# Where an attention's loads stand in its slots, and when the first expert's weights are fetched

## The chip, the cores and the metric

The kernel runs on one core of one Trainium2 chip. The metric is the time of one execution on the device in microseconds (us). TensorE multiplies matrices, VectorE, ScalarE and GpSimd do the rest of the arithmetic, and SyncE issues most of the transfers between DRAM and the on-chip memory, one after the other in the order in which they were written. In the profile they are PE (with PEld for weight loads), DVE, ACT, POOL and SP.

## The reference

Attention over 8 batches, 8 heads, 576 positions and 64 features a head, whose scores have a causal mask and a bias from cumulative sums; then a mixture of 8 experts, where a token takes its own best expert or keeps that of the token before it.

```python
scores = scale * np.matmul(q, k.transpose(0, 1, 3, 2))
bias = -(cum[:, :, :, None] - cum[:, :, None, :])          # cum: running sum of max(s, 0)
scores = np.where(causal, -1000000000.0, scores + np.minimum(bias, 0.0))
attn = np.exp(scores - np.max(scores, axis=-1, keepdims=True))
attn = attn / (np.sum(attn, axis=-1, keepdims=True) + 1e-09)
x = np.matmul(attn, v)                                      # heads side by side: (B, S, 512)
...
e = fresh_e if s == 0 or local_gate[b, s] < 0.5 else prev_e # fresh_e: argmax of x @ w_gate
out[b, s] = p[e] * (np.maximum(x[b, s] @ w1[e], 0.0) @ w2[e])   # 512 -> 1024 -> 512
```

## The kernel before, in words

The order of work is written out by hand: the program's engines run their instructions in the order of the code. The attention takes two heads as one pair (32 pairs in all), and two pairs as one slot, `m` = 0 to 15. A slot does this on TensorE:

- the scores of its two pairs, in three units each (`scores`, line 1128, tile `ps`), each unit followed by an exponential on ScalarE (line 1129, tile `e`);
- half-block products (`values_halves`, line 1197) and the half-block scores of the next slot's two pairs (`scores_halves`, line 1146, tile `ph`), which read q and k of the next slot;
- the products with the values of the first pair (`values`, line 1185, into `po`) and of the second (into `pb`), in two parts each; after each part VectorE takes the reciprocals of the sums (`evacuate`, line 1207, tile `recs`) and scales.

After every fourth slot the finished batches' tokens get their router logits, and in the slots that follow their expert is worked out and GpSimd scatters their rows to a table in DRAM (line 364, `table`). From slot 14 on the experts' first two units of tokens are fetched back from that table (`experts.fetch`, line 583, tile `xq`), and after slot 15 the experts run: layer 1 of unit 0 first (line 782, tile `hp`).

The inputs of a slot are loaded two slots ahead. Slot `m` loads q and k (288 KB each) and v (320 KB each) of the pairs 2m + 4 and 2m + 5: `load_v` (line 1027, tile `va`) and `qk_part` (line 1274, tiles `kb`, `qb`). q and k have four buffers each, v has six. The function `transfers` gives a slot's loads, each under the name of a place. `let_go` issues the load that waits under a place, and holds it until the instruction that ended there is through (`held` adds that as a dependency):

- `e{u}{n}`: the exponential of unit `u` of the slot's first (n = 0) or second (n = 1) pair; `e21` is the last of the slot;
- `h`: after the half-block products, with the slot's last exponential as the instruction that is waited for;
- `x0`, `x1`: the reciprocals of the first pair's two parts; `y0`, `y1`: those of the second pair's.

All of them are issued by SyncE, so one that waits holds up those behind it. Also on SyncE are, in slot 2, a small array `ends` written to DRAM and read back twice into `wend` (lines 1093 and 1095, placed between `x1` and `y0`), four stores of padding rows (line 203), and in slot 14 the fetches of units 0 and 1 (placed after the first pair's scores).

The first expert's first-layer weights are one tile `w1b` of 2 MB, loaded in four quarters of 512 KB (`experts.load(0, 0, i, behind)`, line 573). Quarter `i` is the `i`-th quarter of the contraction of 512, so the first output block of layer 1 needs all four.

Of the kernel before, what the change touches and what calls it, by code (L numbers as in the profile page):

```python
# [23 lines left out]
NPAIR = B * HP  # L24
# [963 lines left out]
def attention(ctx, tc, q, k, v, s, wx, ident, recs, wend, router, experts):  # L988
# [32 lines left out]
    def load_v(n, behind=None):  # L1021

        if n >= NPAIR:
            return
        b, hp = divmod(n, HP)
        va = vs[n] = p_v.tile([P, NB, 2, DH], F32, name="va")
        held(tc, nc.sync.dma_start(va.rearrange("p c h d -> p (c h d)"), v[b, hp].rearrange("p c h d -> p (c h d)")), behind)
# [207 lines left out]
    for g in range(NG - 1):  # L1235
        m = HP * GB // 2 * (g + 1)
# [9 lines left out]
        for c in range(NC):  # L1246
# [3 lines left out]
            i, p = places[c]  # L1250
# [3 lines left out]
    m = NPAIR // 2  # L1254
# [14 lines left out]
    def qk_part(n, what):  # L1269
        def load(behind):  # L1270
            b, hp = divmod(n, HP)
            to = p_in.tile([P, S], F32, name=what + "b")
            ins.setdefault(n, [None, None])["qk".index(what)] = to
            held(tc, nc.sync.dma_start(to, (q, k)["qk".index(what)][b][:, hp]), behind)
        return load

    def v_part(n):
        return lambda behind: load_v(n, behind)

    def transfers(m):  # L1280

        n = 2 * m + NV
        k0, q0, k1, q1 = (qk_part(n + i, x) for i in range(2) for x in "kq")
        if m == 0:
            return {"e11": v_part(4), "h": k0, "x0": q0, "x1": k1, "y0": q1}
        if m == 1:
            return {"e00": v_part(5), "e10": v_part(6), "e20": k0, "e11": q0, "h": k1, "x0": q1, "x1": v_part(7)}
        of = {"e00": v_part(n), "e20": v_part(n + 1), "e11": k0, "h": q0, "x0": k1, "x1": q1} if n < NPAIR else {}
        i = m - NPAIR // 2 + 5
        if 0 <= i < 4:  # L1290
            of["y1"] = lambda behind: experts.load(0, 0, i, behind)
        return of

    waiting = {}

# [4 lines left out]
    for m in range(NPAIR // 2):  # L1300
        pair = 2 * m, 2 * m + 1
        waiting = transfers(m)
        for n in pair:
            for u in range(len(UNITS)):
# [623 lines left out]
```

## Time and profile before

| | |
|---|---|
| median of 3 runs | 692.24 us (689.48 to 693.06) |
| the profiled execution | 693.14 us |
| its span, first to last instruction | 691.2 us |
| granted TensorE clock | 0.998 |
| TensorE busy | 672.4 us (97%) |
| DMA queues: loads (q1), scatters and stores (q0), instructions (q8, q14) | 58.4%, 7.6%, 0.7% of 16 DMA engines' span |

A row of the engine timeline gives the start and the length in us, the engine, the line, the operation, the tiles written and read, the shape, the count, and in brackets how long the engine had been idle and what released it; "issue" there is a wait that no other engine's or transfer's signal ended. A row of the chain (the work that ended last, traced back from the end) gives start, length and what ran. A row of the table by stretches gives the stretch, its length, each engine's busy time and number of instructions in it (in the order PE, PEld, DVE, ACT, POOL), the granted clock, the mean busy share of the 16 DMA engines, and GB/s.

### The profile page before, as it was taken

What the parts mean: (1) busy time and instruction counts of PE and PEld (TensorE: products, weight loads), DVE (VectorE), ACT (ScalarE), POOL (GpSimd) and SP (SyncE); (2) the same over time, 40 slices, a digit from 0 to 9 for tenths busy, and PEclk for the clock granted to TensorE, in tenths of its full rate; (3) what the DMA queues carried; (4) which work ended last, traced back from release to release, by engine and by line L of the source; (5) the groups of instructions that cost most, each with busy time, mean ns of one, the idle gap of its engine ahead of it and who ended that gap; (6) DMA issues with size and microseconds to landing.
All of it is one profiled execution on the core that took longest, in us unless ns stands there. A gap on an engine that the chain in (4) does not pass through costs nothing.

```text
span 691.2 us, 19171 instructions
## 1 busy us (share of the span) xinstructions
PE 672.4 (97%) x7837; PEld 582.7 (84%) x7837; DVE 523.1 (76%) x979; ACT 198.1 (29%) x368; POOL 385.6 (56%) x547
## 2 busy tenths in 40 slices
PE   8999999999999999999999999999999999999995
PEld 7887888878888899999998999999697897779984
DVE  4664867876875797989989997786587786679762
ACT  4554636355332121121211212212121122212121
POOL 3552367777685858647455465645444373525642
PEclk9999999999999999999999999999999999999999
DMA  7664566777668978499848546464987979856001
GB/s 258 194 209 150 165 199 181 228 215 222 178 213 347 328 260 288 131 362 364 285 155 288 193 154 264 129 265 123 362 289 303 409 261 325 267 249 257 31 13 39
DMA packets 54968, 158.18 MB, mean 229 GB/s; under 512 B 11156, under 2 KB 31636, under 8 KB 49111
## 3 DMA queue, kind: packets, MB, share of 16 engines
q1 hardware_dynamic: 47751, 136.52, 58.4%
q0 software_dynamic: 6880, 20.10, 7.6%
q8 instruction: 64, 1.05, 0.6%
q14 instruction: 33, 0.27, 0.1%
q10 hardware_dynamic: 240, 0.25, 0.1%
HBM read 136.21 MB, written 20.85 MB: 227 GB/s over the span
## 4 chain that ended last, share of the span: by engine, by line
PE 90%; DVE 4%; issue 2%; DMA 1%; POOL 1%; ACT 1%; POOLq 0%; DVEq 0%
PE p L692 28%; PE p L688 27%; PE ps L1128 11%; PE po L1185 6%; PE pb L1185 6%; PE hp L782 4%; PE yp L805 2%; PE hp L773 2%; PE lp L231 1%; PE ph L1146 1%; DVE wt L618 1%; PE po L1197 1%; DMA qb<-in_q_dram 1%; PE pb L1197 1%; POOL out_dram L757 1%
## 5 line engine op out<-in xcount | busy, mean ns | idle before, releaser
L692 PE MATMUL p<-w2b,hT 128*128 128x256 f32 (+1 forms) x720 | 165.0, 380 | 3.2 <-DVE w2b L618 2.4
L692 PEld LDWEIGHTS p<-w2b,hT 128*128 128x128 f32 (+1 forms) x720 | 132.8, 187 | 26.1 <-issue 5.2
L688 PE MATMUL p<-xT,w1b 128*128 128x128 f32 (+1 forms) x1280 | 151.1, 275 | 0.9 <-DVE w1b L618 0.9
L688 PEld LDWEIGHTS p<-xT,w1b 128*128 128x128 f32 x1280 | 147.9, 192 | 3.5 <-issue 1.6
L1129 ACT ACTIVATE e<-ps 128x768 f32<-128x768 f32 (+1 forms) x96 | 76.3, 885 | 60.4 <-PE ps L1128 60.4
L757 POOL DMA_INDIRECT out_dram<-y,gi x38 | 45.3, 1191 | 81.7 <-ACT y L716 72.8
L717 ACT ACTIVATE hT<-hT 128x512 f32<-128x512 f32 (+1 forms) x64 | 39.0, 615 | 154.8 <-DVE hT L712 154.8
L716 ACT ACTIVATE y<-y,gi 128x256 f32<-128x256 f32 (+1 forms) x72 | 35.5, 506 | 166.1 <-DVE y L712 154.0
L1128 PE MATMUL ps<-qb,kb 64*128 64x384 f32 (+4 forms) x516 | 76.9, 444 | 0.2 <-ACT e L1129 0.2
L669 POOL TENSOR_TENSOR hT<-hT,hS 128x512 f32<-128x512 f32 (+1 forms) x18 | 26.4, 1467 | 87.4 <-PE p L692 87.3
L1128 PEld LDWEIGHTS ps<-qb,kb 64*128 64x128 f32 x516 | 47.6, 188 | 27.1 <-ACT e L1129 10.4
L692 PE MATMUL p<-wt,hS 128*128 128x256 f32 (+1 forms) x288 | 68.1, 379 | 0.2 <-DVE wt L618 0.2
L364 POOL DMA_INDIRECT table<-xb,idx x54 | 55.7, 1032 | 15.6 <-issue 13.5
L1112 POOL TENSOR_SCALAR_AFFINE_SELECT e<-e 128x128 f32<-128x128 f32 (+1 forms) x96 | 38.8, 417 | 44.2 <-ACT e L1129 43.5
L688 PE MATMUL p<-xS,wt 128*128 128x128 f32 (+1 forms) x512 | 62.4, 275 | 0.0
L692 PEld LDWEIGHTS p<-wt,hS 128*128 128x128 f32 (+1 forms) x288 | 53.7, 187 | 8.9 <-PE p L692 0.6
L688 PEld LDWEIGHTS p<-xS,wt 128*128 128x128 f32 x512 | 59.7, 192 | 0.0
L1185 PE MATMUL pb<-vg,e 128*64 128x66 f32 x1280 | 42.0, 223 | 3.7 <-issue 3.7
L1185 PEld LDWEIGHTS pb<-vg,e 128*64 128x64 f32 x1280 | 39.7, 138 | 4.8 <-issue 4.7
L1185 PE MATMUL po<-vg,e 128*64 128x66 f32 x1280 | 41.4, 223 | 1.1 <-issue 1.1
L1185 PEld LDWEIGHTS po<-vg,e 128*64 128x64 f32 x1280 | 38.9, 138 | 2.5 <-issue 1.3
L1105 DVE TENSOR_TENSOR vg<-va,wk 128x256 f32<-128x256 f32 x64 | 37.7, 652 | 0.0
(290 smaller groups left out, 984.7 us busy)
## 6 DMA issues: line engine op xcount, KB each, us to landing
w2b<-in_w_dram SPq DMA_DIRECT2D x23, 2048.0 KB, 12.2
w1b<-in_w_dram SPq DMA_DIRECT2D x22, 2048.0 KB, 14.0
va<-in_v_dram SPq DMA_DIRECT2D x32, 320.0 KB, 3.5
kb<-in_k_dram SPq DMA_DIRECT2D x31, 288.0 KB, 3.0
qb<-in_q_dram SPq DMA_DIRECT2D x31, 288.0 KB, 4.9
xq<-table SPq DMA_DIRECT2D x60, 130.0 KB, 3.1
w1b<-in_w_dram SPq DMA_DIRECT2D x4, 512.0 KB, 4.7
xq<-table SPq DMA_DIRECT2D x12, 113.8 KB, 12.8
```

The lines of the kernel that those rows point to most:

```text
L364: put = self.nc.gpsimd.indirect_dma_start(out=self.halves, in_=src, element_offset=0, in_offset=None, out_offset=bass.IndirectOffsetOnAxis ...
L688: mm(ps[:, m * h : m * h + h], lhsT=b[:, k, m * P : m * P + P], rhs=a[:, k, :], start=m == 0 and k == 0, stop=m == FK // 2 - 1 and k == n - 1)
L692: mm(ps[:h, : D // 2], lhsT=a[:, k, :], rhs=b[:, k, :], start=k == 0, stop=k == n - 1)
L716: return nc.scalar.mul(to, to, gi[:h, r, 1:2]).ins
L717: return nc.scalar.activation(to, to, Act.Relu).ins
L757: put = nc.gpsimd.indirect_dma_start(out=self.out[:, :], out_offset=bass.IndirectOffsetOnAxis(ap=gi.bitcast(I32)[:m, n, 0:1], axis=0), in_ ...
L782: mm(ps, lhsT=self.ws[ls[0]][0][:, k, c * P : c * P + P], rhs=xT[:, k, :w], start=(k == 0), stop=(k == DK - 1))
L1105: nc.vector.tensor_tensor(vg[:, to].rearrange("p c h e -> p (c h) e")[:, :, :DH], va[:, :c].rearrange("p c h e -> p (c h) e"), wk[:, n, to ...
L1112: nc.gpsimd.affine_select(out=ap, in_=ap, compare_op=Alu.is_ge, fill=0.0, base=base, pattern=n, channel_multiplier=-1)
L1128: mm(ps[:, h, at : at + z - a], lhsT=kb[d, key : key + P], rhs=qb[d, a:z], start=True, stop=True)
L1129: exps[n, u] = nc.scalar.activation(e[:, :, : WIDTH[u]], ps, Act.Exp, scale=scale).ins
L1185: of = mm(po[part][d, j - a, :], lhsT=weights_of(n, c, j, h), rhs=vgs[n % NV][:, c if j < 2 * G1 else G1 + c, h, :], start=(first and i == ...
```

## The change

Only the table in `transfers` changes. A slot's loads are given other places, and the four quarters of the first expert's weights, one in each of the slots 11 to 14 at `y1`, are now all in slot 14, which has no loads of q, k and v.

```diff
         n = 2 * m + NV
         k0, q0, k1, q1 = (qk_part(n + i, x) for i in range(2) for x in "kq")
-        if m == 0:
-            return {"e11": v_part(4), "h": k0, "x0": q0, "x1": k1, "y0": q1}
-        if m == 1:
-            return {"e00": v_part(5), "e10": v_part(6), "e20": k0, "e11": q0, "h": k1, "x0": q1, "x1": v_part(7)}
-        of = {"e00": v_part(n), "e20": v_part(n + 1), "e11": k0, "h": q0, "x0": k1, "x1": q1} if n < NPAIR else {}
-        i = m - NPAIR // 2 + 5
-        if 0 <= i < 4:
-            of["y1"] = lambda behind: experts.load(0, 0, i, behind)
-        return of
+        if m < 2:
+            return {"e21": v_part(n), "h": k0, "x0": q0, "x1": k1, "y0": q1, "y1": v_part(n + 1)}
+        if n < NPAIR:
+            return {"e21": v_part(n), "h": v_part(n + 1), "x0": k0, "x1": q0, "y0": k1, "y1": q1}
+        parts = ("h", "x0", "x1", "y0") if n == NPAIR else ()
+        return {x: lambda behind, i=i: experts.load(0, 0, i, behind) for i, x in enumerate(parts)}
```

On TensorE, VectorE, ScalarE and GpSimd every instruction stands where it stood; only SyncE's queue differs. In an ordinary slot even its order is the same, and what differs is the engine that each load waits for. These are SyncE's rows of slot 4 before (in brackets the semaphores, DMAHW of an earlier transfer, and the engine whose instruction lets the load go: Activation is ScalarE's exponential, DVE VectorE's reciprocal):

```order
L1027 DMA va<-in_v_dram 128x640 [waits DMAHW1_49,Activation_49]
L1027 DMA va<-in_v_dram 128x640 [waits DMAHW2_49,Activation_49]
L1274 DMA kb<-in_k_dram 128x576 [waits DMAHW3_49,Activation_49]
L1274 DMA qb<-in_q_dram 128x576 [waits DMAHW4_49,Activation_49]
L1274 DMA kb<-in_k_dram 128x576 [waits DMAHW5_49,DVE_49]
L1274 DMA qb<-in_q_dram 128x576 [waits DMAHW6_49,DVE_49]
```

And the same six now:

```order
L1027 DMA va<-in_v_dram 128x640 [waits DMAHW1_49,Activation_49]
L1027 DMA va<-in_v_dram 128x640 [waits DMAHW2_49]
L1274 DMA kb<-in_k_dram 128x576 [waits DMAHW3_49,DVE_49]
L1274 DMA qb<-in_q_dram 128x576 [waits DMAHW4_49,DVE_49]
L1274 DMA kb<-in_k_dram 128x576 [waits DMAHW5_49,DVE_49]
L1274 DMA qb<-in_q_dram 128x576 [waits DMAHW6_49,DVE_49]
```

Both v now wait for the slot's one last exponential, and all of q and k for the reciprocals.

In slot 2, where SyncE also has the transfers of `ends`, `wend` and the padding (`table<-pad`), its rows before were these, from the slot's second k on:

```order
L1274 DMA kb<-in_k_dram 128x576 [waits DMAHW2_49,DVE_49]
L1274 DMA qb<-in_q_dram 128x576 [waits DMAHW3_49,DVE_49]
L1093 DMA ends<-ends 64x9 [waits DMAHW4_49,Pool_49]
L1095 DMA wend<-ends 64x288 [waits DMAHW5_49,DMAHW4_49]
L1095 DMA wend<-ends 64x288 [waits DMAHW6_49]
L203 DMA table<-pad 128x260 [waits DMAHW7_49,Pool_49]
```

And now, from the first q on:

```order
L1274 DMA qb<-in_q_dram 128x576 [waits DMAHW1_49,DVE_49]
L1093 DMA ends<-ends 64x9 [waits DMAHW2_49,Pool_49]
L1095 DMA wend<-ends 64x288 [waits DMAHW3_49,DMAHW2_49]
L1095 DMA wend<-ends 64x288 [waits DMAHW4_49]
L1274 DMA kb<-in_k_dram 128x576 [waits DMAHW5_49,DVE_49]
L1274 DMA qb<-in_q_dram 128x576 [waits DMAHW6_49,DVE_49]
L203 DMA table<-pad 128x260 [waits DMAHW7_49,Pool_49]
```

The second k and q moved behind `ends` and the two reads of `wend`, the first of which waits for the transfer of `ends`.

In slot 14, after the fetch of unit 1, SyncE had one quarter left before (the loads of 128x4096 are those of the expert stage):

```order
L583 DMA gi<-table 128x2x2
L573 ISA
L573 DMA w1b<-in_w_dram 128x1024
L556 TENSOR_LOAD a0of
L573 ISA
L573 DMA w1b<-in_w_dram 128x4096
```

Now it has the read of the expert's number (`a0of`) and all four:

```order
L583 DMA gi<-table 128x2x2
L556 TENSOR_LOAD a0of
L573 ISA
L573 DMA w1b<-in_w_dram 128x1024
L573 ISA
L573 DMA w1b<-in_w_dram 128x1024
L573 ISA
L573 DMA w1b<-in_w_dram 128x1024
L573 ISA
L573 DMA w1b<-in_w_dram 128x1024
L556 TENSOR_LOAD a0of
```

The three quarters that stood behind the loads of the slots 11, 12 and 13 have left those places.

## Prediction

> **What bounds the kernel now.** I read the page first, then the engine waits of TensorE, then its timeline at the waits, then counts of its instructions up to them.
>
> ```profile
> PE 672.4 (97%) x7837; PEld 582.7 (84%) x7837; DVE 523.1 (76%) x979; ACT 198.1 (29%) x368; POOL 385.6 (56%) x547
> q8 instruction: 64, 1.05, 0.6%
> PE 90%; DVE 4%; issue 2%; DMA 1%; POOL 1%; ACT 1%; POOLq 0%; DVEq 0%
> ```
>
> TensorE is busy for 672.4 of 691.2 us and holds 90% of the chain that ended last, so the change can win only what makes TensorE wait in the attention (the first 201 us; the experts keep their order). Its waits there are nearly all of one kind:
>
> ```profile
> PE pb L1185 <- issue: 3.7, 6, 1.3
> PE po L1185 <- issue: 1.1, 2, 0.7
> ```
>
> These are eight stalls, 4.8 us in all, inside the products of the values, where no data released the engine ("issue"). Three of them in its timeline (start, us, what, idle before):
>
> ```profile
> 52.98 1.51 PE L1185 MATMUL pb<-vg,e 128*64 128x66 f32 x45 [1.17 <-issue]
> 148.78 1.44 PE L1185 MATMUL pb<-vg,e 128*64 128x66 f32 x42 [1.28 <-issue]
> 197.54 0.86 PE L1185 MATMUL po<-vg,e 128*64 128x66 f32 x22 [0.33 <-issue]
> ```
>
> What they wait for shows in a count. The table by stretches gives TensorE's matmuls and weight loads from the start up to a time (the x after PE and PEld):
>
> ```profile
> 0.00:47.80 47.80, 45.51 (x975) 37.07 (x979) 26.39 (x60) 24.85 (x41) 23.22 (x82) 1.00 0.68 215
> 0.00:51.90 51.90, 49.52 (x1106) 40.88 (x1107) 29.31 (x67) 26.07 (x43) 25.37 (x85) 1.00 0.70 221
> 0.00:60.70 60.70, 57.24 (x1231) 46.72 (x1235) 33.90 (x75) 31.04 (x50) 27.88 (x91) 1.00 0.66 211
> 0.00:143.90 143.90, 139.68 (x3263) 114.57 (x3267) 96.20 (x250) 74.26 (x131) 78.85 (x190) 1.00 0.63 196
> 0.00:147.60 147.60, 143.28 (x3392) 117.96 (x3392) 99.28 (x264) 76.01 (x135) 82.11 (x197) 1.00 0.64 198
> 0.00:197.30 197.30, 190.71 (x4536) 156.76 (x4536) 135.97 (x366) 100.09 (x177) 118.65 (x268) 1.00 0.65 200
> ```
>
> The three stalls come at instructions 2213, 6784 and 9072. The distances, 4571 and 2288, are 18 and 9 times 254. The q8 row has 64 packets in 1.05 MB, 16.4 KB each, for 15,674 matmuls and weight loads: TensorE gets its program in blocks of some 254 of these, each one packet on queue 8, and it stalls at a border whose next block is late. In the DMA view the block's packet starts within 50.6 to 50.7, 146.5 to 146.6 and 195.2 to 195.3 us, and for a block that came in time within 61.2 to 61.3 us:
>
> ```profile
> q8 instruction: 1, 0.02, 58.2%
> q8 instruction: 1, 0.02, 60.5%
> q8 instruction: 1, 0.02, 67.1%
> q8 instruction: 1, 0.02, 63.4%
> ```
>
> TensorE resumed 2.3, 2.2 and 2.3 us after the first three. The block before the stall at 51.8 began at about 47.8 (254 instructions earlier), so its fetch started 2.8 us in: 2.8 + 2.3 is 1.1 us more than the 4.0 us that the block lasted, and 1.17 was measured. From 143.9 it is 2.6 + 2.2 against 3.6: 1.2, measured 1.28. The block that began at 60.7 had its fetch after 0.5 us and no stall. What differs is the traffic of the other queues (last columns: DMA share, GB/s):
>
> ```profile
> 48.10:50.60 2.50, 2.50 (x91) 2.50 (x87) 1.60 (x4) 0.70 (x2) 1.96 (x3) 1.00 0.90 280
> 144.00:146.50 2.50, 2.50 (x110) 2.43 (x101) 2.26 (x11) 1.43 (x4) 2.16 (x6) 1.00 0.87 220
> 61.00:61.20 0.20, 0.20 (x16) 0.19 (x8) 0.00 (x0) 0.00 (x0) 0.00 (x0) 1.00 0.12 46
> ```
>
> The late fetches stood behind 2.5 us of DMA at 90% and 87%; the quick one met 12%. The loads of q, k and v delay TensorE's instructions.
>
> [...] In this trace the borders cost 4.8 us.
>
> **The change, term by term.** Only SyncE's queue has another order; the other engines run the same rows.
>
> *The block fetches of the slots before the last.* The loads stood at the first exponential of a slot, its fourth, fifth and last, and the first two sums. They now start at the last exponential and end with the last sums.
>
> ```profile
> 43.45 4.75 ACT L1129 ACTIVATE e<-ps 128x1024 f32<-128x1024 f32 x6 [0.86 <-PE ps L1128]
> 46.66 0.97 SPq L1027 DMA_DIRECT2D va<-in_v_dram  x2
> 47.72 0.38 SPq L1274 DMA_DIRECT2D kb<-in_k_dram  x1
> 48.23 0.36 SPq L1274 DMA_DIRECT2D qb<-in_q_dram  x1
> ```
>
> In slot 3 the block at 47.8 met four loads issued from 46.66 to 48.23. Now the first v may go at 48.2, where the exponentials end, and moves no byte before the block's fetch is asked for. The backlog falls on the next block, which holds the scores and is long: the one from 51.8 lasts to 60.7, 8.9 us, against 3 + 2.3 that its fetch needs. Seven of the stalls, 4.8 - 0.33 = 4.45 us, lie in these slots. Ends: all 4.45 go, or none. I take it that each leaves 0.2 us, since a block that begins just after the last exponential still meets the two v loads: 7 x 0.2 = 1.4 us. Net -3.05.
>
> *The second k and q of slot 2.* They now stand on SyncE behind the two reads of wend, which wait for a DRAM round trip:
>
> ```profile
> 39.98 0.53 SPq L1093 DMA_DIRECT2D ends<-ends  x1
> 43.31 1.11 SPq L1095 DMA_DIRECT2D wend<-ends  x2
> 44.52 2.04 SPq L203 DMA_DIRECT2D table<-pad  x4
> 47.35 0.58 PE ph L1146 x40
> ```
>
> So k goes at 44.5 (where the first pad went) and q at 45.0; the half blocks' scores of slot 3 (ph) use them from about 47.4, and the stall ahead of them (0.25) that goes makes it 47.1. Landing, by the page's list of issues (KB each, median us):
>
> ```profile
> kb<-in_k_dram SPq DMA_DIRECT2D x31, 288.0 KB, 3.0
> qb<-in_q_dram SPq DMA_DIRECT2D x31, 288.0 KB, 4.9
> w1b<-in_w_dram SPq DMA_DIRECT2D x4, 512.0 KB, 4.7
> ```
>
> By the k row q is there at 48.0, a wait of 0.9 us; by the q row, whose loads stood behind others, at 49.9, 2.8 us. The queue is quiet here, so I take 1.0. The pads move behind them and nobody is near to needing those.
>
> *The second q of the other slots.* It is let go by the last sums (the reciprocal below ends at 115.45) and needed by ph of the next slot:
>
> ```profile
> 115.23 0.22 DVE L1207 RECIPROCAL recs<-pb 128x10 f32<-128x10 f32 x1 [1.13 <-PE pb L1185]
> 120.24 0.58 PE ph L1146 x40
> ```
>
> That is 4.8 us of cover; with 3.0 to land 1.8 us are left. Cost 0.1 us for a slot where the four releases come close together; ends 0 and 5 (a rival below). The v loads, now later by up to 4 us, are used by VectorE at the end of the slot: in slot 3 the values end at 54.5 (52.98 + 1.51), 6.3 us after the last exponential, and a v is to be there in the time of a k (3.0) with another ahead of it (about 1 more): 0.
>
> *The expert's quarters.* Three leave the slots 11 to 13 (that gain is in the first term), and all four go in slot 14:
>
> ```profile
> 183.48 2.54 SPq L583 DMA_DIRECT2D xq<-table  x4
> 187.14 3.06 SPq L583 DMA_DIRECT2D xq<-table  x4
> 191.05 10.44 SPq L573 DMA_DIRECT2D w1b<-in_w_dram  x2
> 201.02 5.38 PE hp L782 x24
> 179.00:180.00 1.00, 1.00 (x10) 0.52 (x8) 1.00 (x3) 1.00 (x3) 0.91 (x1) 1.00 1.00 303
> ```
>
> Their places in slot 14 have passed when SyncE is through with fetching two units' rows at 190.9, so they go together, from 191.3 to about 193. A lone quarter fills the DMA engines at 303 GB/s, so 2.1 MB take 6.9 us from 192.3, to 199.2, and with the scatters that share these engines to about 200.5. The first product of unit 0 (hp, 201.02) needs all four: 0.1 us, ends 0 and 2. The block from 193.7 now meets the burst. Before, with one quarter, its fetch came 1.5 us in and the stall was 0.33. The longest wait for a fetch seen is 2.8 us, which makes a stall of 1.6; at 2.3 it is 1.1. I take 1.1, so +0.8; ends -0.3 and +4 (a rival).
>
> Sum: -3.05 + 1.0 + 0.1 + 0.1 + 0.8 = -1.05 us. The profiled execution took 693.14 us (span 691.2), 0.9 above the median of 692.24; the difference counts from the median: **691.2 us**. The experts are to pass it on, TensorE being the bound there as well.
>
> **Rivals.**
> 1. *All block stalls go and the late loads are in time.* For it: the quick fetch in the quiet stretch. -4.8 + 0.5 = -4.3, or 687.9.
> 2. *The stalls stay and move.* The loads still take the same share of the slot; two v loads stand together where two single ones were, and products of values now meet them. Then only the costs are left: 692.24 + 2.0 = 694.2. [...] Against it: the 12% row.
> 3. *The burst holds the instructions.* If the block from 193.7 stands behind all four quarters, it is fetched at 199.2 and there at 201.5, against 197.2 needed: 4.3 us instead of 1.1, 694.4. [...] No row here has such a burst beside a fetch.
> 4. *Slower: the second q is late in every slot.* If it takes over 4.8 us to land, ph waits in the nine slots where no router product lies before it. At 5.4 us: 9 x 0.6 = 5.4, or 696.6. For it the 4.9 of the q row; against it, that the queue ahead of it is now short.
>
> **Chances.** Forecast 0.45 (its own range 689.5 to 693), rival 1 0.15, rival 2 0.20, rival 3 0.12, rival 4 0.08. A measurement tells about 0.5%, 3.5 us, from no change: faster takes most of rival 1 and a little of the forecast, 0.15; slower rival 4 and the tails of 2 and 3, 0.10; the rest, 0.75, is the same. The range 688.4 to 694.8 leaves out most of rival 1 and rival 4.
>
> **What would show it.** Right: the rows "pb L1185 <- issue" and "po L1185 <- issue" fall from 4.8 to about 2.5 us, with the longest now near 194 to 198 us; ph of slot 3 waits about 1 us at 47; hp does not wait for w1b. Wrong: as many such stalls as before at other borders (rival 2), a ph wait in each slot (rival 4), one of over 3 us near 197 (rival 3), or none.

## The result and the profile after

The changed kernel took 698.23 us (median of ten executions, 695.41 to 702.73); the kernel before, beside it, 691.87 (ten, 689.48 to 696.42). The ratio is 1.0088 [1.006, 1.0116]: the change costs about 6 us, where 691.2 was forecast with a range up to 694.8. The profiled execution took 698.63 us, span 696.9 (before 693.14 and 691.2).

The page after, its row of busy times and the chain by engine:

```profile
PE 675.8 (97%) x7837; PEld 586.8 (84%) x7837; DVE 524.6 (75%) x979; ACT 198.3 (28%) x368; POOL 385.5 (55%) x547
PE 80%; DMA 7%; DVE 6%; issue 3%; ACT 1%; POOL 1%; SPq 1%; POOLq 0%; DVEq 0%; ACTq 0%
```

TensorE runs the same 7837 matmuls and is busy 3.4 us longer (675.8 against 672.4), which no order of loads should do. In the chain DMA has grown from 1% to 7%; that share counts transfers in full and is no loss of that size (27.0 us of it are two loads of expert weights late in the program, one of 18.58 and one of 8.44 us). TensorE's waits, with the total, the number and the longest:

```profile
PE ph L1146 <- DMA qb<-in_q_dram: 3.2, 2, 2.9
PE po L1185 <- issue: 2.5, 1, 2.5
PE ph L1146 <- issue: 1.0, 2, 0.8
PE pb L1185 <- issue: 0.8, 2, 0.4
```

The block stalls of the slots before the last have gone from 4.45 us to 1.8 (the last two rows), much as forecast. What is new is one wait for q and one stall of 2.5 us:

```profile
50.54 0.92 PE L1146 MATMUL ph<-qb,kb 64*64 64x64 f32 x24 [2.85 <-DMA qb<-in_q_dram]
202.16 0.86 PE L1185 MATMUL po<-vg,e 128*64 128x66 f32 x22 [2.47 <-issue]
```

And both are followed by slow products. From the chain (start, length, what ran), the pieces around the two places, with an undisturbed slot's products between them:

```profile
46.67 3.74 DMA qb<-in_q_dram
50.54 0.92 PE ph L1146 x24
51.91 4.79 PE po L1185 x84
...
67.33 2.60 PE po L1185 x84
69.93 2.45 PE pb L1185 x84
...
199.69 2.47 issue
203.20 4.05 PE pb L1185 x83
207.25 5.38 PE hp L782 x24
```

The same 84 products take 4.79 us behind the wait for q and 2.60 in the next slot; those of `pb` take 4.05 behind the stall and 2.45 elsewhere. The table by stretches shows why, in the column after the five engines, the granted clock (then DMA share, GB/s):

```profile
46.30:49.71 3.41, 1.39 (x42) 1.08 (x38) 3.00 (x5) 2.01 (x3) 1.69 (x4) 1.00 0.79 239
49.71:53.12 3.41, 2.58 (x64) 2.48 (x66) 0.09 (x1) 0.70 (x1) 0.77 (x1) 0.50 0.95 284
53.12:56.54 3.42, 3.42 (x68) 3.42 (x66) 0.54 (x2) 0.00 (x0) 0.78 (x1) 0.50 0.42 129
...
199.90:203.31 3.41, 1.15 (x39) 1.15 (x40) 0.57 (x3) 0.00 (x0) 0.97 (x1) 1.00 1.00 397
203.31:206.73 3.42, 3.42 (x70) 3.42 (x66) 1.19 (x4) 0.00 (x0) 2.32 (x4) 0.50 0.31 119
```

The clock changed at 49.71, 56.54, 203.31 and 206.73 us; these times lie on one grid of 3.41 us, and the stretches are cut along it. In the stretch from 46.30 TensorE was busy for 1.39 of 3.41 us (idle 0.59), in that from 199.90 for 1.15 (idle 0.66), and the clock then stood at half, for two stretches and for one.

The sum from this profile, in us: wait for q +2.85, slow `po` +2.19 (4.79 - 2.60), the stall +2.14 (2.47 against 0.33 before), slow `pb` +1.60 (4.05 - 2.45), together +8.78. Of the 4.45 of stalls in the slots before the last there are 0.8 + 1.0 left, and 0.35 of a second wait for q: -2.3. That is +6.5. The experts began at 207.25 instead of 201.02, 6.2 later, and the span is 5.7 longer.

### The profile page after: what moved, and what is told of

It is laid out like the page before. It is cut to its first block, busy times and chain, and to the rows that moved or that the text cites. A ratio compares the mean times of both kernels' runs of the same rounds, so it can differ in the third digit from the quotient of the medians.

```text
span 696.9 us, 19157 instructions
## 1 busy us (share of the span) xinstructions
PE 675.8 (97%) x7837; PEld 586.8 (84%) x7837; DVE 524.6 (75%) x979; ACT 198.3 (28%) x368; POOL 385.5 (55%) x547
## 4 chain that ended last, share of the span: by engine, by line
PE 80%; DMA 7%; DVE 6%; issue 3%; ACT 1%; POOL 1%; SPq 1%; POOLq 0%; DVEq 0%; ACTq 0%
PE p L692 27%; PE p L688 23%; PE ps L1128 8%; PE po L1185 6%; PE pb L1185 5%; PE hp L782 4%; DMA w1b<-in_w_dram 3%; PE hp L773 2%; DMA qb<-in_q_dram 2%; PE lp L231 1%; PE ph L1146 1%; DMA w2b<-in_w_dram 1%; DVE wt L618 1%; PE yp L805 1%; PE po L1197 1%
## 5 line engine op out<-in xcount | busy, mean ns | idle before, releaser
L1185 PE MATMUL po<-vg,e 128*64 128x66 f32 x1280 | 43.2, 229 | 2.5 <-issue 2.5
L1185 PEld LDWEIGHTS po<-vg,e 128*64 128x64 f32 x1280 | 40.9, 143 | 3.8 <-issue 2.6
```

Source lines behind the costliest of these rows:

```text
L1185: of = mm(po[part][d, j - a, :], lhsT=weights_of(n, c, j, h), rhs=vgs[n % NV][:, c if j < 2 * G1 else G1 + c, h, :], start=(first and i == ...
```

## The experiments

Each ratio is to the kernel before on the same chip: median 694.17 (35 executions) for the kernels with `ends` last, with the quarters in four slots, with both edits and with the late k and q alone, 693.94 (24) for the others.

**The small write `ends` behind the second q of slot 2.** Changed kernel, with

```diff
-    plan(2, 3, range_ends)
+    plan(2, 4, range_ends)
```

> The changed kernel with one edit: the transfers of ends and wend stand behind the slot's last k and q instead of ahead of them. Theory (late loads, then half clock): the changed kernel loses 2.85 us at the half-block scores of slot 3, where k and q of slot 2 come late, and 2.2 us right after, where the granted clock is 0.50 and the 84 products of po take 4.79 instead of 2.60 us. With both gone the time falls by 5.0 us to about 693.2, the wait at ph in slot 3 and the stretch at half clock near 50 to 57 us are gone, and the ones near 200 us stay. Rival (the loss is DMA traffic that slows the products of slot 3 themselves, not the wait): po stays at 4.8 us and the time falls by 2.9 at most, to 695.4.

Measured: 693.6 us (12), ratio 0.9985 [0.996, 1.001]. The changed kernel, run again as a control without an edit, gave 700.3 (6), 1.0075 [1.0047, 1.0103], so by the two ratios, which come from two chips, this line is worth some 6 us (5.0 were expected). What the control was expected to do (the windows of the clock are the stretches of 3.41 us in the table above):

> The changed kernel itself again, beside the experiments of this group. If the two losses add up as the pairs of the first group say (order of ends: 4.0 us between the kernels with spread quarters, quarters: 2.8 us between the kernels with ends last), it stands 6.8 us above the kernel with both edits, about 697.6 where the kernel before takes 694.2. Where the profile falls in the windows of the clock decides how much of it is half clock.

SyncE's queue in the changed kernel's profile, whose lengths of a row are issuing, not landing:

```profile
40.66 0.52 SPq L1093 DMA_DIRECT2D ends<-ends  x1
44.84 1.11 SPq L1095 DMA_DIRECT2D wend<-ends  x2
46.04 0.54 SPq L1274 DMA_DIRECT2D kb<-in_k_dram  x1
46.67 0.38 SPq L1274 DMA_DIRECT2D qb<-in_q_dram  x1
```

`ends` goes at 40.66, the first read of `wend` waits 4.2 us for it, and k and q stand behind both; q lands at 50.41 (46.67 + 3.74 in the chain above). With `ends` behind them, the chain of this kernel has

```profile
46.72 0.58 PE ph L1146 x40
47.53 2.60 PE po L1185 x84
```

no wait, and `po` at full speed. The burst's stall is still there, here 3.40 us:

```profile
197.91 1.48 PE L1185 MATMUL po<-vg,e 128*64 128x66 f32 x22 [3.40 <-issue]
```

**The quarters back in four slots.** Changed kernel, with

```diff
-        if n < NPAIR:
-            return {"e21": v_part(n), "h": v_part(n + 1), "x0": k0, "x1": q0, "y0": k1, "y1": q1}
-        parts = ("h", "x0", "x1", "y0") if n == NPAIR else ()
-        return {x: lambda behind, i=i: experts.load(0, 0, i, behind) for i, x in enumerate(parts)}
+        of = {"e21": v_part(n), "h": v_part(n + 1), "x0": k0, "x1": q0, "y0": k1, "y1": q1} if n < NPAIR else {}
+        i = m - NPAIR // 2 + 5
+        if 0 <= i < 4:
+            last = of.get("y1", lambda behind: None)
+            of["y1"] = lambda behind: (last(behind), experts.load(0, 0, i, behind))
+        return of
```

> The changed kernel with its four quarters of weights put back to the last sums of slots 11 to 14, behind that place's q. Theory: the stall of 2.47 us at the block border near 199.7 us goes back to 0.3, and with it the 1.6 us that the 84 products of pb lose at half clock: 3.7 us less, about 694.5. Rival (the burst costs nothing beyond the 0.8 us forecast, and the rest near 200 us comes from the fetches of the units' rows and the scatters): a stall of over 1.5 us stays there, and the time falls by under 1.5 us.

Measured: 694.77 us (12), 1.0013 [0.9989, 1.0036]. The long stall near 200 us is down to 0.57; the wait for q in slot 3 is still there, and in this execution it brought no half clock:

```profile
49.60 0.58 PE L1146 MATMUL ph<-qb,kb 64*64 64x64 f32 x24 [2.61 <-DMA qb<-in_q_dram]
50.35 2.55 PE L1185 MATMUL po<-vg,e 128*64 128x66 f32 x80
```

The block stalls of the slots before the last, however, are back at 4.3 us:

```profile
PE pb L1185 <- issue: 4.3, 7, 1.4
PE po L1185 <- issue: 0.6, 1, 0.6
```

So the time lies near the forecast, but in part by two things that were not forecast and that work against each other: no half clock behind the wait, and these stalls.

**Both edits.**

> Both edits together. Theory: the two losses are independent, 5.0 + 3.7 = 8.7 us less than the changed kernel, about 689.5, that is 2.4 us faster than the kernel before, since the stalls at the block borders of slots 4 to 13 (3.0 us before, 0.8 in the changed kernel) stay away. Rival (the new places of the loads are themselves slower): still above 691.9. Second rival (new stalls appear at other borders once the phase has moved): 690.5 to 692.

Measured: 690.78 us (12, 688.19 to 692.84), 0.9953 [0.9934, 0.9973]. It is the only version whose interval lies wholly below the kernel before, and this is what the places of the loads of q, k and v are worth when `ends` stands last: 3.4 us by the medians. Its waits for instructions are 2.4 us, where the kernel before has 4.8, so the stalls of the two profiles account for 2.4 of the 3.4 (the profiled execution is its fastest, 688.19):

```profile
PE pb L1185 <- issue: 1.7, 3, 1.3
PE po L1185 <- issue: 0.7, 1, 0.7
```

From this kernel back, spreading the quarters is worth 2.8 us (693.6 to 690.78) and moving `ends` 4.0 (694.77 to 690.78), together 6.8; the changed kernel lies 9.5 above (its control, on the other chip). The difference of 2.7 is not much more than the uncertainty of the control (about 1.9 us either way), so it isn't shown that the two costs fail to add up. A part may be the clock: its mean was 0.9972 with both edits, 0.9958 with either one, 0.9920 in the control, and the control's loss is some 1.7 us more than the sum of the two others (an estimate, each difference from 0.9972 taken over 697 us).

**The late k and q alone.** Kernel before, with its second k and q of slot 2 behind `ends` and `wend`:

```diff
+        if m == 2:
+            of["y0"], of["y1"] = of.pop("x0"), of.pop("x1")
```

> The kernel before with one thing of the change alone: in slot 2 the second k and q are let go at the second pair's sums, and so stand behind ends and wend. Theory: the wait at ph in slot 3 (2 to 3 us) and the half clock behind it (1.5 to 2.2 us) appear, the border stall of 1.17 us in slot 3 goes, since the wait gives its block time: 2.5 to 4.5 us slower than before, 694.4 to 696.4. Rival (the wait is short, 1.0 us as forecast, and the clock stays): within 0.5 us of before.

Measured: 695.54 us (12), 1.0015 [0.9989, 1.0038]. There is no wait for q here at all, although the order on the queue is the changed kernel's:

```profile
39.22 0.53 SPq L1093 DMA_DIRECT2D ends<-ends  x1
41.19 1.11 SPq L1095 DMA_DIRECT2D wend<-ends  x2
42.40 1.12 SPq L1274 DMA_DIRECT2D kb<-in_k_dram  x1
43.62 0.38 SPq L1274 DMA_DIRECT2D qb<-in_q_dram  x1
```

The round trip of `ends` took 2.0 us, not 4.2, and began 1.4 earlier. In the kernel before, the slot's v and first k and q are issued well ahead of `ends`; in the changed kernel they go just ahead of it. So the place behind `wend` costs the wait only together with the late release of the other four loads. That the time lies in the range expected is luck: neither the wait nor the half clock came. In this profile the block stalls are 6.5 us in all, 4.8 in that of the kernel before, and the stall of slot 3, which was to go, is 1.83.

**The wait filled with products.** Changed kernel, with 14 products whose results nobody reads (28 matmuls in the trace) on TensorE just ahead of the half-block scores that wait for q:

```diff
+            if i and warm:
+                q8, k8 = ins[2 * m]
+                for _ in range(warm):
+                    mm(full[heads[0], 0, NH * DH :], lhsT=k8[heads[0], :DH], rhs=q8[heads[0], : 512 - NH * DH],
+                       start=True, stop=True)
+                warm = 0
```

> The changed kernel with 14 products (64 x 192, of data that is there, into columns of the bank that nothing reads) on TensorE ahead of the half-block scores of slot 3 that wait for k and q. k and q come as late as before, so nothing is won by the wait itself. Theory (half clock because of the idle wait): TensorE is busy over most of the 2.9 us, the granted clock stays 1.00 from 44 to 58 us, the 84 products of po take 2.60 us, and the kernel is up to 2.2 us faster than the changed one, by how often its wait falls so that the clock drops. Rival (the slow products are due to the traffic, or the profile shows them too long): po stays at 4.8 us, and the time is the changed kernel's or up to 2.4 us more. The 28 extra instructions move all later block borders, so stalls elsewhere can change by 1 us.

Measured: 697.45 us (10), 1.0053 [1.0034, 1.0072], 2.9 us below the changed kernel on the same chip, with intervals that overlap. Its stretches from 46.9 us:

```profile
46.90:51.00 4.10, 4.10 (x34) 3.37 (x26) 1.70 (x3) 0.72 (x2) 0.83 (x2) 1.00 0.97 287
51.00:54.50 3.50, 3.50 (x128) 3.37 (x128) 0.63 (x2) 0.70 (x1) 1.55 (x2) 1.00 0.79 212
```

and its chain:

```profile
46.99 4.32 PE ph L1147 x27
52.11 2.60 PE po L1192 x84
```

The traffic is no lighter (DMA share 0.97, and 0.79 while `po` runs; in the changed kernel `po` was still slow in a stretch with 0.42), TensorE does more work, and `po` takes 2.60 at clock 1.00 instead of 4.79. So the slow products are the clock's doing and not the DMA's, and what lowered the clock was an idle TensorE (for 0.59 of the stretch ahead in the changed kernel, not at all here). The filling itself was too long (4.3 us for a wait of 2.85), which by the profiles gives back some 1.5 of the 2.19. The 2.9 of the medians is more than what is left, so it isn't this wait alone: the stall in slot 15 of this profile is 2.11 us and has no half clock behind it. The mean granted clock of the ten executions is 0.9961, that of the control's six 0.9920.

The inserted matmuls also show that the stalls go by a count of instructions. In the kernel before, and in those with the quarters spread, with the late k and q and with the burst alone, the stall of slot 3 comes after 35 products of `pb`; here, with 28 more matmuls ahead, it comes after 7.

**The burst alone.** Kernel before, with only the quarters moved into slot 14:

```diff
-        i = m - NPAIR // 2 + 5
-        if 0 <= i < 4:
-            of["y1"] = lambda behind: experts.load(0, 0, i, behind)
+        parts = ("h", "x0", "x1", "y0") if n == NPAIR else ()
+        of.update({x: lambda behind, i=i: experts.load(0, 0, i, behind) for i, x in enumerate(parts)})
```

> The kernel before with the other part of the change alone: the four quarters in slot 14, all other loads where they were. Theory: the block border in the products of slot 15 stalls for 2.4 to 3.4 us instead of 0.3, in part with half clock behind it (1.6 us); the border stalls that quarters caused in the slots 11 to 13 (1.28 and 0.73 us among them) shrink by about 1: 1.5 to 4 us slower than before. Rival (the burst matters only with the new places of the other loads): within 1 us of before, and no stall over 1 us near 200 us.

Measured: 697.17 us (9), 1.0047 [1.0028, 1.0066]. With the burst alone the kernel is 3.2 us slower; the stall behind it took 2.57 us in the profile, much as in the changed kernel. The profiled execution, 1.9 us above the median, has half clock after it too:

```profile
199.29:202.71 3.42, 1.19 (x41) 1.05 (x36) 1.78 (x8) 0.00 (x0) 2.15 (x5) 1.00 0.74 288
202.71:206.12 3.41, 3.07 (x56) 3.07 (x58) 1.02 (x4) 0.00 (x0) 0.36 (x2) 0.50 0.05 12
```

The other executions mostly have not: the mean granted clock of the nine is 0.9971, that of the kernel before 0.9970. And the stalls of the earlier slots did not shrink by 1 us, as was expected, but grew in this profile to 6.9 us, although three quarters had left the slots 11 to 13:

```profile
PE pb L1185 <- issue: 6.7, 8, 1.9
PE po L1185 <- issue: 2.8, 2, 2.6
```

What makes these vary so much was not settled, so the 3.2 us are not shown to be the one long stall alone.

**Two quarters instead of four.** Changed kernel with `ends` last, quarters 0 and 1 in slots 12 and 13 and two in slot 14:

```diff
-    plan(2, 3, range_ends)
+    plan(2, 4, range_ends)
-            return {"e21": v_part(n), "h": v_part(n + 1), "x0": k0, "x1": q0, "y0": k1, "y1": q1}
-        parts = ("h", "x0", "x1", "y0") if n == NPAIR else ()
-        return {x: lambda behind, i=i: experts.load(0, 0, i, behind) for i, x in enumerate(parts)}
+            of = {"e21": v_part(n), "h": v_part(n + 1), "x0": k0, "x1": q0, "y0": k1, "y1": q1}
+            if m in (12, 13):
+                of["y1"] = lambda behind: (q1(behind), experts.load(0, 0, m - 12, behind))
+            return of
+        parts = ("h", "x0") if n == NPAIR else ()
+        return {x: lambda behind, i=i: experts.load(0, 0, 2 + i, behind) for i, x in enumerate(parts)}
```

> The changed kernel with ends last, and two of the four quarters at the last sums of slots 12 and 13, two in slot 14. It tells how the wait for a block grows with the burst. If a fetch waits for about two quarters that stand ahead of it, however many follow (3.4 and 4.4 us of waiting with four), the stall is 1.5 to 3 us, little less than with four. If it waits for all that stand ahead, it is half of that with four or less, 0.7 to 1.5 us. With one it was 0.3 to 0.7. Time: between the kernel with four (693.6) and that with one (690.8).

Measured: 692.86 us (12, 688.81 to 697.96), 0.998 [0.9954, 1.0005]. In the profile the stall is as long as with four quarters, in fact longer, and above both ranges that were expected:

```profile
200.08 0.86 PE L1185 MATMUL po<-vg,e 128*64 128x66 f32 x22 [3.80 <-issue]
200.95 2.44 PE L1185 MATMUL pb<-vg,e 128*64 128x66 f32 x78
```

With the four together it was 2.11 (filled wait), 2.47 (changed), 2.57 (burst alone), 3.40 (`ends` last), 3.64 (control); with one, 0.33 to 0.73. The 4 KB packets of `w1b` in the traces, 128 to a quarter, tell what a fetch stands behind. From the start of a block to the packet of the next, 1.6 to 2.5 quarters moved in the five profiles with four, 1.9 in the one with two (all that there was), 0.6 to 0.8 in those with one. So a fetch waited behind about two quarters, however many followed, as far as one execution with two can tell. The products behind this stall ran at full speed, although it is the longest of all:

```profile
194.70:198.12 3.42, 1.58 (x55) 1.44 (x49) 2.15 (x9) 0.00 (x0) 2.54 (x6) 1.00 0.79 299
198.12:201.53 3.41, 1.45 (x48) 1.45 (x50) 0.34 (x2) 0.00 (x0) 0.02 (x1) 1.00 0.17 57
```

A border of the clock's grid fell into it at 198.12: TensorE was idle for 0.54 of the one stretch and 0.58 of the other, and neither was enough.

## Why the prediction was wrong

It said 691.2; 698.23 came. The steps that failed are the sizes of two terms, the wait for q in slot 3 and the stall in slot 15, and the half clock behind both, for which it had no term. Step by step, with the sizes of the profiled execution:

- *The block fetches of the slots before the last* (-3.05): right in the main. The stalls fell by 2.65 (4.45 to 1.8), and the version with both edits is 3.4 us faster than before. Over all profiles, one execution each, these stalls are 4.45, 5.8 and 6.9 us with the old places of the loads and 1.7 to 2.5 in six of seven with the new. The seventh, the kernel with spread quarters, has 4.3, so rival 2, by which the stalls stay and move, came true there and not in the others. That these stalls cost time is shown by the 4.8 us of them before and the 3.4 won by moving loads.
- *The second k and q of slot 2* (+1.0): the mechanism was right, the size wrong: 2.85, just above the upper end of 2.8. I took the time of `wend` from the profile of before (43.31), so that k went at 44.5; it went at 46.04. Before, the slot's other loads had gone ahead of `ends` by some time; the change lets four of them go just ahead of it, so the round trip became 4.2 us instead of 3.3, and started 0.7 later. The queue that I called quiet was not: q took 3.74 to land instead of the 3.0 taken. Moving `ends` away removed the wait, and the old release of the other loads did so too.
- *The second q of the other slots* (+0.1): small, as forecast; one such wait, 0.35, in slot 14 (two, 1.7 us, in the kernel with two quarters). Rival 4 did not come.
- *The expert's quarters, the landing for* `hp` (+0.1): right by luck. The experts did not wait for them at their start, but the quarters' packets took from 195.5 to 205.6, 10.1 us, where 192.3 to 200.5 was forecast. Begun at 192.3 they would have ended at 202.4 at that pace, 1.4 us after `hp` was to start; that TensorE itself came 6.2 us late hid it.
- *The block from 193.7* (+0.8, a stall of 1.1): mis-sized. It took 2.47 there, and 2.11 to 3.80 in the kernels with two or four quarters in slot 14. I took the longest fetch seen beside loads of q, k and v (2.8 us) for a bound; behind quarters the packet came some 3.6 us after its block began (199.8 against 196.2, the latter counted in the trace), in the DMA view of 199.8 to 199.9. Rival 3 had the sign but the wrong rule: the packet came when 239 of the 512 packets of `w1b` had started, and two quarters would have cost less than four, which they did not.

```profile
q8 instruction: 1, 0.02, 60.4%
```

- *Missing: the clock.* No term and no rival had it, though the granted clock stands in every row that I quoted. It is 3.79 us of this profile (2.19 + 1.60). Over all executions it is less: the mean granted clock was 0.9927 in the changed kernel's ten and 0.9970 in 24 of the kernel before, which over 697 us makes about 3.0 us (an estimate that counts the whole span alike). Without it the time would have been some 695.2, about the upper end of the range (0.4 above it): the two terms that were sized too small bring it that far by themselves.

The experts passed the delay on, as assumed: 6.2 us at their start, 5.7 at the end.

## What to carry to other kernels

A wait of TensorE is not priced by its length: where it left the engine idle for some 0.6 of one 3.41 us stretch of the clock's grid, work at half speed could follow (2.19 us lost behind the wait of 2.85, 1.60 behind that of 2.47), so two waits cost 9 here while eight of 0.6 on average had cost 5. Before moving loads behind a point, look for a round trip through DRAM on the same queue and price it with the loads that now stand ahead of it, not with the time it had (4.2 us here, 3.3 before). Large loads were better one at a time between other work than in a burst (by 2.8 us with `ends` last): the late instruction block's packet came when 239 of the burst's 512 had started, and in the one profile with two quarters the stall, 3.80 us, was already as bad as with four (2.11 to 3.64).

## What the runs showed of the hardware that was not expected

**The clock went by a grid of 3.41 us, not by the length of a wait.** In the attention of the ten profiles half clock followed stretches with TensorE idle for 0.59 (a busy time of 1.39 us), 0.61, 0.65, 0.66, 0.66 and 0.97, and did not follow 0.54, 0.56, 0.58, less than these and, in the execution with the filled wait, 0.59 (busy 1.40). The two at 0.59 lie so close that the border may be put there in these runs. To come back took more: after a stretch at half clock in which TensorE was idle for 0.24, 0.30 or 0.46 the next was at half clock too, after one with 0.10 or less it was not. That is why it lasted two stretches in slot 3 of the changed kernel and one in slot 15. The stretch with 0.97 is that of the kernel with `ends` last, where a wait of 3.40 us happened to fill one whole stretch:

```profile
194.41:197.83 3.42, 0.10 (x3) 0.00 (x0) 0.78 (x3) 0.00 (x0) 1.21 (x3) 1.00 1.02 409
197.83:201.24 3.41, 3.33 (x60) 3.33 (x62) 1.28 (x4) 0.00 (x0) 0.62 (x2) 0.50 0.20 76
```

Waits of 2.47 and 2.85 us were followed by a clock of 0.50, and one of 3.80, split by a border, was not. The grid was not tied to the program's start: in the two profiles of the changed kernel the clock first dropped at 49.71 and at 48.78 us, 0.93 us apart, which is no whole number of stretches. So the same wait may cost some 2 us more in one execution than in the next (an estimate: 2.19 us were lost behind the wait of 2.85, none behind the 2.61 with the quarters in four slots); that fits the scatter of the changed kernel (clocks of 0.988 to 0.996 in its ten executions, the slowest time with the lowest), but the alignment of each of them was not profiled.

**An instruction block waited behind about two large loads.** A quarter moved as 128 packets of 4 KB. From the start of a block to the packet of the next, 1.6 to 2.5 quarters moved in the profiles with four together and 1.9 in the one with two; the stalls were 2.11 to 3.80 us behind two or four and 0.33 to 0.73 behind one. Why it was about two, no run here shows.

**A block was 256 instructions, not 254.** The table by stretches, from which the 254 was counted, leaves out the instructions of TensorE's sequencer. Counted in the trace with these, the block stalls of the kernel before lie a multiple of 256 apart to within one: they come at 1730, 2241, 4545, 6338, 6850, 7361, 8130 and 9154.

**A tiny write to DRAM took 2.0 us with few loads around it and 4.2 us with the slot's four ahead of it on its queue,** from its issue to that of the read behind it, by the two listings of SyncE above. In the other profiles with four loads just ahead of it it was 3.8 to 4.8, in those where the second k and q go ahead of it too and so spread the loads out, 2.9 to 3.3.
